# Softmax sums of an attention layer: ones products in four column groups of 32 in place of tile additions

## The chip, the cores and the metric

The kernel runs on one core of one Trainium2 chip. The metric is the device time of one execution in microseconds (us); lower is better. One execution was also taken with the hardware profiler, and all rows below come from it.

## The reference

Three layers follow each other on 896 tokens (2 batches of 448), 768 wide:

```python
scores = cap * np.tanh(scale * (q @ k.T) / cap)          # 24 heads, 448 x 448, head 64 wide
attn = np.exp(scores - max)
attn = attn / (attn.sum(axis=-1, keepdims=True) + 1e-9)
x = attn @ v                                             # then 896 x 768
x = moe(x)       # RMS norm, two products 768 -> 1536, SiLU gate, product 1536 -> 768
return moe2(x)   # product 768 -> 2048, PReLU, product 2048 -> 768
```

The change touches `attn.sum` alone: how the sum over keys is made and brought to the division.

## The kernel before, in words

**Tiling.** Two heads make a pair, and there are 12 pairs. Scores stand with keys on the 128 partitions and the 448 queries along the free dimension. A head has 448 keys: three tiles of 128 and a tail of 64. The tails of both heads share one tile, so a pair has seven tiles of exponentials in two bursts: b = 0 with four tiles, b = 1 with two full tiles and the shared tail. So there are 24 bursts, n = 0 to 23, burst n being (pair n // 2, half n % 2).

**One burst.** `qk` (L188) makes the scores of two groups of tiles on TensorE, each operand split in a high and a low part (`hi`, `lo`, made by `prep`, L174 and L175, on VectorE). `soft` does tanh (L198) and exp (L200) on ScalarE. `pv` (L211) multiplies with V; head 0 goes to columns 0 to 63 of the array and head 1 to 64 to 127. The PSUM pool of the scores has two buffers, one per group.

**The sums before.** `add_tiles` adds the full tiles of a pair to one tile per head on GpSimd (L223 after b = 0, L226 after b = 1), `add_tails` adds the halves of the tail tile on VectorE (L232), and `sums` multiplies the result with ones on TensorE (L238, one float32 product per head, 64 columns each; a float32 product is two passes, so four MATMULs a pair). `evac_u` copies the sum out of PSUM with the epsilon added (L270) and lays one row per head into `gt` by DMA (L273, on SyncE's queue). `recip` (L281 to L289) takes the reciprocal for a group of two pairs on 64 partitions, splits it in two parts and lays them into `r2` by two DMAs. `norm` spreads `r2` over partitions by a product (L314), multiplies (L315), and then squares and adds for the RMS norm, mostly on GpSimd (L296, L300, L304). The last pair has its own way: `sums_now` (L247) and `norm_now` (L322 to L324).

**Order.** The schedule is written by hand. Iteration n of the loop issues `qk` and `soft` of burst n, then `pv` of burst n - 1, then what `at(n, ...)` has put down for slot n, in the order in which it was put down. Every engine takes its instructions in this order, so a waiting instruction holds up all that its engine has behind it. Before, pair i has `add_tiles` in slots 2i + 1 and 2i + 2, `evac_o` (L262, frees the product with V) in slot 2i + 2, `add_tails` and then `sums` in slot 2i + 3, `evac_u` in slot 2i + 4, `recip` in slot 2i + 5 (every second pair), `norm` from slot 2i + 6. `prep` of pair i + 1 and the loads of pairs i + 1 (V) and i + 2 (Q and K) stand in slot 2i. Eight weight units are converted in between (L102 and L119 on ScalarE, L106 and L123 on VectorE, L114 on GpSimd). Slot 19 holds `rms(0)` (L333 to L337), slots 20 to 23 the six `xnorm` of batch 0 (L350 to L356, VectorE). After the last burst the products of the first layer begin (L368).

Of the kernel before, what the change touches and what calls it, by code (L numbers as in the profile page):

```python
# [7 lines left out]
F32 = mybir.dt.float32  # L8
# [6 lines left out]
ALU = mybir.AluOpType  # L15
PSUM = bass.MemoryType.PSUM

P = 128
B, H, S, D = 2, 12, 448, 64
# [13 lines left out]
RMS_EPS = 1e-6  # L33
SM_EPS = 1e-9
RP = 16
K3 = KD // 2
G1 = K1 // 2
G2 = K2N // 4
# [15 lines left out]
def attn_moe_kernel(ctx: ExitStack, tc: tile.TileContext, units, qk_in, v, sel, w, gvec, alpha, cap, out):  # L54
    nc = tc.nc
# [7 lines left out]
    sb = att.enter_context(tc.tile_pool(name="sb", bufs=2))  # L63
# [8 lines left out]
    eps_t = aconst.tile([P, 1], F32, name="eps_t")  # L72
    rms_b = aconst.tile([P, 1], F32, name="rms_b")
    ones = aconst.tile([P, P], F32, name="ones")
    half = aconst.tile([P, 2, D], F32, name="half")
# [80 lines left out]
    NPAIR = B * NP  # L156
# [22 lines left out]
    st, pt = {}, {}  # L179
# [19 lines left out]
            n += w  # L199
        nc.scalar.activation(out=t[:, :n], in_=t[:, :n], func=AF.Exp, scale=cap_t)  # L200

    oo, us, ut, ee, gt = {}, {}, {}, {}, {}

    def pv(i, b):
        t, vv = pt[i, b], vt[i]
# [9 lines left out]
        if b == 1:  # L215
            del hi[i], lo[i], vt[i]

    def add_tiles(i, b):

        t = pt[i, b]  # L220
        if b == 0:
            ut[i] = sb.tile([P, 2, S], F32, tag="ut", name="ut", bufs=2)
            nc.gpsimd.tensor_tensor(out=ut[i], in0=t[:, 0:2], in1=t[:, 2:4], op=ALU.add)  # L223
            del pt[i, 0]
        else:
            nc.gpsimd.tensor_tensor(out=ut[i], in0=ut[i], in1=t[:, 0:2], op=ALU.add)  # L226

    def add_tails(i):
        t = pt.pop((i, 1))
        for h in range(2):  # L230
            rows = slice(h * D, h * D + D)
            nc.vector.tensor_tensor(out=ut[i][rows, h], in0=ut[i][rows, h], in1=t[rows, 2], op=ALU.add)  # L232

    def sums(i):
        us[i] = ps_r.tile([P, 512], F32, tag="u", name="us")
        u = ut.pop(i)
        for h in range(2):
            nc.tensor.matmul(us[i][h * D:h * D + D, :S], ones[:, :D], u[:, h], start=True, stop=True)  # L238

    def sums_now(i):  # L240

        us[i] = ps_r.tile([P, 512], F32, tag="r", name="us")
        a, c = pt[i, 0], pt[i, 1]
        tiles = [a[:, 0], a[:, 1], a[:, 2], a[:, 3], c[:, 0], c[:, 1], c[:, 2], c[:, 2]]
        for n, t in enumerate(tiles):
            h = n % 2
            nc.tensor.matmul(  # L247
                us[i][h * D:h * D + D, :S], half[:, h] if n > 5 else ones[:, :D], t, start=n < 2, stop=n > 5,
                skip_group_check=True,
            )  # L250
# [4 lines left out]
    members = [[i, i + 1] for i in range(0, NPAIR - 2, 2)] + [[NPAIR - 2]]  # L255
# [8 lines left out]
    def evac_u(i):  # L264

        n, j = group[i]
        if j == 0:
            gt[n] = sb.tile([4 * RP, S // RP], F32, tag="gt", name="gt")
        u = sb.tile([P, S], F32, tag="us", name="us")
        nc.vector.tensor_scalar_add(u, us.pop(i)[:, :S], eps_t)  # L270
        for h in range(2):
            r0 = RP * (2 * j + h)
            nc.sync.dma_start(  # L273
                out=gt[n][r0:r0 + RP, :], in_=u[h * D:h * D + 1, :].rearrange("o (p s) -> o p s", p=RP)
            )

    def recip(n):
        t = gt.pop(n)
        w = 2 * len(members[n])
        m = slice(0, w * RP)  # L280
        nc.vector.reciprocal(out=t[m], in_=t[m])  # L281
        th = sb.tile([4 * RP, S // RP], F32R, tag="th", name="th")
        tl = sb.tile([4 * RP, S // RP], F32R, tag="tl", name="tl")
        nc.vector.tensor_copy(th[m], t[m])
        nc.vector.tensor_tensor(out=tl[m], in0=t[m], in1=th[m], op=ALU.subtract)
        rr = r2[n % 2]
        for r0, x in ((0, th), (32, tl)):
            row = rr[r0:r0 + w].rearrange("r (p s) -> r p s", p=RP)
            nc.sync.dma_start(out=row.bitcast(F32), in_=x[m].bitcast(F32))  # L289

    def square(i):
        b, p = divmod(i, NP)
        x = xf[b][:, p, :]
        if p == 0:
            s2[b] = [sb.tile([P, S], F32, tag="s2", name="s2", bufs=1)]
            nc.gpsimd.tensor_tensor(out=s2[b][0], in0=x, in1=x, op=ALU.mult)  # L296
        else:
            sq = sb.tile([P, S], F32, tag="sq", name="sq", bufs=2)
            if i < NPAIR - 4:
                nc.gpsimd.tensor_tensor(out=sq, in0=x, in1=x, op=ALU.mult)  # L300
            else:
                nc.scalar.activation(out=sq, in_=x, func=AF.Square)
            if p < NP - 1 and i < NPAIR - 2:
                nc.gpsimd.tensor_tensor(out=s2[b][0], in0=s2[b][0], in1=sq, op=ALU.add)  # L304
            else:
                s2[b].append(sq)
# [3 lines left out]
    def norm(i):  # L310
        b, p = divmod(i, NP)
        n, j = group[i]
        rps = ps_r.tile([P, 512], F32, tag="r", name="rps")
        nc.tensor.matmul(rps[:, :S], sel_t[:, j, :], r2[n % 2], start=True, stop=True)  # L314
        nc.vector.tensor_tensor(out=xf[b][:, p, :], in0=ee.pop(i), in1=rps[:, :S], op=ALU.mult)  # L315
        square(i)

    def norm_now(i):

        b, p = divmod(i, NP)  # L320
        u = sb.tile([P, S], F32, tag="us", name="us")
        nc.vector.tensor_scalar_add(u, us.pop(i)[:, :S], eps_t)  # L322
        nc.vector.reciprocal(out=u, in_=u)
        nc.vector.tensor_tensor(out=xf[b][:, p, :], in0=oo.pop(i)[:, :S], in1=u, op=ALU.mult)  # L324
        square(i)
# [3 lines left out]
    def rms(b):  # L329
        ms = ps_o.tile([P, 512], F32, tag="o", name="ms")  # L330
        parts = s2.pop(b)
        for n, t in enumerate(parts):
            nc.tensor.matmul(ms[:, :S], ones, t, start=n == 0, stop=n == len(parts) - 1)  # L333
        spare[b] = xpool.tile([P, K3, S], F32, tag="B22h", name="spare")
        rstd[b] = spare[b][:, 2]
# [6 lines left out]
    def first_operand(name):  # L342
        if name not in oper:
            oper[name] = [xpool.tile([P, K3, S], F32R, tag=f"{name}{p}", name=f"x{p}") for p in "hl"]
        return oper[name]

    def xnorm(i):
# [5 lines left out]
        if b == 0:  # L353
            h, l = first_operand("B21" if p >= K3 else "B11")
            nc.vector.tensor_copy(h[:, p % K3, :], x)
            nc.vector.tensor_tensor(out=l[:, p % K3, :], in0=x, in1=h[:, p % K3, :], op=ALU.subtract)  # L356

# [3 lines left out]
    def product(ps, u, name, first, rows=(0, 1)):  # L361

        wh, wl = h_t[u], l_t[u]
        xh, xl = oper[name]
        for r in rows:
            mm = [(a[:, r * K3 + k, :], x[:, k, :]) for a, x in ((wh, xh), (wl, xh), (wh, xl)) for k in range(K3)]
            for n, (lhs, rhs) in enumerate(mm):
                nc.tensor.matmul(  # L368
                    ps[:, r, :S], lhs, rhs, start=first and n == 0, stop=n == len(mm) - 1,
                    skip_group_check=True,  # L370
                )
# [14 lines left out]
    with tc.manual_schedule():  # L386
# [39 lines left out]
        def at(n, fn, *a):  # L426
            later.setdefault(n, []).append((fn, a))

        NA = len(bursts)
        last = NPAIR - 1  # L430
        for i in range(NPAIR):
            if i < last:
                at(2 * i + 4, evac_u, i)
        for i in range(NPAIR):
            if i < last:
                at(2 * i + 3, add_tails, i)
                at(2 * i + 3, sums, i)
        for i in range(NPAIR):
            at(2 * i, prep, i + 1)
            at(2 * i, load_raw, i + 2)  # L440
            at(2 * i, load_v, i + 1)
            if i < last:
                at(2 * i + 2, evac_o, i)
                for b in range(2):
                    at(2 * i + 1 + b, add_tiles, i, b)
                n, j = group[i]
                if j == len(members[n]) - 1 and n < len(members) - 1:
                    at(2 * i + 5, recip, n)
                    if n < len(members) - 2:
                        for m, i2 in enumerate(members[n]):  # L450
                            at(2 * i + 6 + m, norm, i2)
            if i == NP - 1:
                at(2 * i + 9, rms, 0)
                for m in range(NP):
                    at(2 * i + 10 + m * 2 // 3, xnorm, m)
# [14 lines left out]
        for n in range(NA):  # L470
            i, b = bursts[n]
# [5 lines left out]
            for fn, a in later.pop(n, []):  # L477
                fn(*a)
        sums_now(last)
        pv(*bursts[-1])  # L480
        for n in sorted(later):
# [4 lines left out]
        def pair_tile(pool, tag):  # L486
            return pool.tile([P, 2, 512], F32, tag=tag, name=tag)
# [14 lines left out]
                fn(*a)  # L502
        for g in range(2):
            pa[g] = pair_tile(ps_s, "s")
        norm_now(last)
        norm(last - 3)
        product(pa[0], ("g", 0, "A11"), "B11", True)
        recip(len(members) - 1)
        norm(last - 2)
        w_hi(("g", 0, "S1"))  # L510
        w_lo(("g", 0, "S1"))
# [489 lines left out]
```

## Time and profile before

| | |
|---|---|
| median of 3 runs | 653.34 us (652.91 to 654.76) |
| the profiled execution | 656.73 us |
| its span | 655.0 us |
| mean granted TensorE clock | 0.957 of 2.4 GHz |
| busy: PE, DVE, ACT, POOL | 593.3, 426.4, 341.0, 159.2 us |

The span and the profiled execution's own time differ by the launch, 1.7 us. PE is TensorE, DVE is VectorE, ACT is ScalarE, POOL is GpSimd and SPq is SyncE's queue; PEclk is the clock granted to TensorE as a share of 2.4 GHz, so that 0.5 is 1.2 GHz and a value between the two is a mean over a stretch. Matmuls are pipelined: one starts before the one ahead of it has ended, so the spacing of their starts says more than their durations. Engines work beside each other, so busy times do not add up to the span; the chain of waits is followed back from the last instruction, and only what stands on it sets the end.

### The profile page before, as it was taken

What the parts mean: (1) busy time and instruction counts of PE and PEld (TensorE: products, weight loads), DVE (VectorE), ACT (ScalarE), POOL (GpSimd) and SP (SyncE); (2) the same over time, 40 slices, a digit from 0 to 9 for tenths busy, and PEclk for the clock granted to TensorE, in tenths of its full rate; (3) what the DMA queues carried; (4) which work ended last, traced back from release to release, by engine and by line L of the source; (5) the groups of instructions that cost most, each with busy time, mean ns of one, the idle gap of its engine ahead of it and who ended that gap; (6) DMA issues with size and microseconds to landing.
All of it is one profiled execution on the core that took longest, in us unless ns stands there. A gap on an engine that the chain in (4) does not pass through costs nothing.

```text
span 655.0 us, 7086 instructions
## 1 busy us (share of the span) xinstructions
PE 593.3 (91%) x2793; PEld 481.4 (74%) x2793; DVE 426.4 (65%) x444; ACT 341.0 (52%) x389; POOL 159.2 (24%) x82
## 2 busy tenths in 40 slices
PE   6787766667899999999999999999989989999997
PEld 3233222223577899999999999999979979999996
DVE  4766656669778998777696344597986788613200
ACT  6596554536156465454566254358767687524101
POOL 3425376606050053423100003530233100000000
PEclk9997787778799999999999999999999999999999
DMA  8244321100030244441235437200441342632002
GB/s 267 101 143 131 107 94 49 46 17 2 1 145 1 96 136 154 145 143 50 94 99 193 145 116 266 101 0 1 144 146 49 101 152 87 198 118 104 1 0 85
DMA packets 16461, 65.99 MB, mean 101 GB/s; under 512 B 3500, under 2 KB 4012, under 8 KB 16428
## 3 DMA queue, kind: packets, MB, share of 16 engines
q1 hardware_dynamic: 16140, 65.41, 29.9%
q8 instruction: 22, 0.36, 0.2%
q0 software_dynamic: 144, 0.13, 0.1%
q14 instruction: 11, 0.09, 0.0%
q10 hardware_dynamic: 144, 0.00, 0.0%
HBM read 62.66 MB, written 2.75 MB: 100 GB/s over the span
## 4 chain that ended last, share of the span: by engine, by line
PE 75%; DVE 15%; issue 3%; POOL 3%; ACT 2%; DMA 1%; ACTq 0%; SPq 0%; DVEq 0%; POOLq 0%
PE s L368 17%; PE m L368 14%; PE s L637 5%; PE s L641 5%; PE s L639 5%; PE m L637 5%; PE m L641 5%; PE m L639 5%; PE us L238 3%; PE oo L211 3%; PE s L188 3%; DVE ut L232 2%; DVE b L550 2%; DVE wt L106 2%; DVE lo L175 2%
## 5 line engine op out<-in xcount | busy, mean ns | idle before, releaser
L123 DVE TENSOR_TENSOR wl<-wt,wh 128x768 fp32r<-128x768 f32 x98 | 108.5, 1113 | 96.5 <-ACT wh L119 95.4
L114 POOL TENSOR_TENSOR wt<-wt 128x768 f32<-128x768 f32 x40 | 88.6, 2222 | 253.1 <-DVE wt L106 147.1
L119 ACT CAST wh<-wt 128x768 fp32r<-128x768 f32 x98 | 81.3, 832 | 100.0 <-PE s L639 21.9
L102 ACT CAST top<-raw 128x768 f16<-128x768 bf16 x68 | 72.7, 1076 | 50.2 <-DVE wt L106 37.1
L106 DVE SCALAR_TENSOR_TENSOR wt<-raw,top 128x768 uint32<-128x768 uint32 x68 | 69.7, 1028 | 0.1
L198 ACT ACTIVATE pt<-s,cinv 128x896 f32<-128x896 f32 (+1 forms) x48 | 41.6, 907 | 41.8 <-PE s L188 40.5
L238 PE MATMUL us<-ut,ones 128*64 128x448 f32 x44 | 24.1, 795 | 38.6 <-DVE ut L232 38.6
L368 PE MATMUL s<-xh,wh 128*128 128x448 f32 x222 | 57.6, 368 | 0.9 <-DVE b L550 0.9
L368 PE MATMUL s<-xl,wh 128*128 128x448 f32 x222 | 57.2, 366 | 0.8 <-DVE xl L550 0.8
L368 PE MATMUL s<-xh,wl 128*128 128x448 f32 x222 | 57.1, 366 | 0.0
L637 PE MATMUL s<-ks,wh 128*128 128x448 f32 x176 | 50.8, 368 | 1.1 <-DVE b L878 1.1
L641 PE MATMUL s<-ks,wl 128*128 128x448 f32 x176 | 50.7, 367 | 0.0
L368 PE MATMUL m<-xh,wh 128*128 128x448 f32 x174 | 45.6, 371 | 2.4 <-ACT b L497 1.9
L637 PE MATMUL m<-ks,wh 128*128 128x448 f32 x160 | 45.8, 367 | 0.5 <-DVE b L550 0.5
L641 PE MATMUL m<-ks,wl 128*128 128x448 f32 x160 | 45.6, 366 | 0.0
L368 PE MATMUL m<-xl,wh 128*128 128x448 f32 x174 | 45.3, 369 | 0.0
L368 PE MATMUL m<-xh,wl 128*128 128x448 f32 x174 | 45.2, 369 | 0.0
L368 PEld LDWEIGHTS s<-xh,wh 128*128 128x128 f32 x222 | 41.5, 188 | 5.1 <-ACT wh L119 1.2
L368 PEld LDWEIGHTS s<-xl,wh 128*128 128x128 f32 x222 | 41.6, 188 | 4.5 <-DVE xl L550 1.1
L211 PE MATMUL oo<-pt,vt 128*64 128x448 f32 x192 | 43.6, 573 | 1.4 <-ACT pt L200 1.1
L238 PEld LDWEIGHTS us<-ut,ones 128*64 128x64 f32 x44 | 5.4, 172 | 53.3 <-DVE ut L232 53.3
L368 PEld LDWEIGHTS s<-xh,wl 128*128 128x128 f32 x222 | 41.7, 188 | 3.4
(136 smaller groups left out, 1056.0 us busy)
## 6 DMA issues: line engine op xcount, KB each, us to landing
raw<-w_in SPq DMA_DIRECT2D x68, 768.0 KB, 4.5
rw<-qk_in SPq DMA_DIRECT2D x11, 480.0 KB, 4.3
vt<-v_in SPq DMA_DIRECT2D x12, 256.0 KB, 4.2
out<-o SPq DMA_DIRECT2D x5, 448.0 KB, 2.5
out<-o SPq DMA_DIRECT2D x2, 224.0 KB
gt<-us SPq DMA_DIRECT2D x22, 1.8 KB, 1.7
rw<-qk_in SPq DMA_DIRECT2D x1, 256.0 KB
rw<-qk_in SPq DMA_DIRECT2D x1, 224.0 KB
```

The lines of the kernel that those rows point to most:

```text
L102: nc.scalar.copy(top_of[u].bitcast(F16)[:, 1::2], raw_t[u].bitcast(BF16)[:, 4:4 * UW + 4:4])
L106: nc.vector.scalar_tensor_tensor(out=f_t[u].bitcast(U32), in0=raw_t.pop(u).bitcast(U32)[:, 1:2 * UW + 1:2], scalar=13, in1=top_of.pop(u), ...
L114: nc.gpsimd.tensor_tensor(out=t, in0=f_t[a], in1=f_t[b], op=op)
L119: nc.scalar.copy(h_t[u], f_t[u].rearrange("p (k m) -> p k m", m=P))
L123: nc.vector.tensor_tensor(out=l_t[u], in0=f_t[u].rearrange("p (k m) -> p k m", m=P), in1=h_t[u], op=ALU.subtract)
L198: nc.scalar.activation(out=t[:, n:n + w], in_=st.pop((i, g))[:, :w, :S], func=AF.Tanh, scale=cinv)
L211: nc.tensor.matmul(oo[i][h * D:h * D + D, :S], vv[:, 2 * c + h, :], t[:, n, :], start=c == 0, stop=c == 3, skip_group_check=True,)
L238: nc.tensor.matmul(us[i][h * D:h * D + D, :S], ones[:, :D], u[:, h], start=True, stop=True)
L368: nc.tensor.matmul(ps[:, r, :S], lhs, rhs, start=first and n == 0, stop=n == len(mm) - 1, skip_group_check=True,)
L637: nc.tensor.matmul(dst[l], wh[:, o, :], xh[l], start=first, stop=False)
L639: nc.tensor.matmul(dst[l], wh[:, o, :], xl[l], start=False, stop=False)
L641: nc.tensor.matmul(dst[l], wl[:, o, :], xh[l], start=False, stop=fin)
```

## The change

The ones product is taken from the exponentials themselves. Eight products per pair (the tail tile twice, with weights that are one for the half of its head and zero for the other) go to four groups of 32 columns: head 0 to columns 0 and 32, head 1 to columns 64 and 96, so that each head has two partial sums. `add_tiles` and `add_tails` are gone. `sums` moves from slot 2i + 3 to 2i + 2, `evac_u` from 2i + 4 to 2i + 3, `recip` from 2i + 5 to 2i + 4. `evac_u` copies without the epsilon and issues four DMAs a pair for two; `recip` adds the two parts and the epsilon in one more VectorE instruction on 64 partitions. The last `recip` moves ahead of `norm_now`.

```diff
-    def add_tiles(i, b):
...
-            nc.gpsimd.tensor_tensor(out=ut[i], in0=t[:, 0:2], in1=t[:, 2:4], op=ALU.add)
-            del pt[i, 0]
-        else:
-            nc.gpsimd.tensor_tensor(out=ut[i], in0=ut[i], in1=t[:, 0:2], op=ALU.add)
-
-    def add_tails(i):
-        t = pt.pop((i, 1))
-        for h in range(2):
-            rows = slice(h * D, h * D + D)
-            nc.vector.tensor_tensor(out=ut[i][rows, h], in0=ut[i][rows, h], in1=t[rows, 2], op=ALU.add)
+    def tiles_of(i):
+        a, c = pt[i, 0], pt[i, 1]
+        return [a[:, 0], a[:, 1], a[:, 2], a[:, 3], c[:, 0], c[:, 1], c[:, 2], c[:, 2]]
 
     def sums(i):
+
         us[i] = ps_r.tile([P, 512], F32, tag="u", name="us")
-        u = ut.pop(i)
-        for h in range(2):
-            nc.tensor.matmul(us[i][h * D:h * D + D, :S], ones[:, :D], u[:, h], start=True, stop=True)
+        for n, t in enumerate(tiles_of(i)):
+            q = n % 2 * D + n // 2 % 2 * Q
+            nc.tensor.matmul(
+                us[i][q:q + Q, :S], half[:, n % 2, :Q] if n > 5 else ones[:, :Q], t, start=n < 4, stop=n > 3,
+                skip_group_check=True,
+            )
+        del pt[i, 0], pt[i, 1]
...
         if j == 0:
-            gt[n] = sb.tile([4 * RP, S // RP], F32, tag="gt", name="gt")
+            gt[n] = sb.tile([4 * RP, 2, S // RP], F32, tag="gt", name="gt")
         u = sb.tile([P, S], F32, tag="us", name="us")
-        nc.vector.tensor_scalar_add(u, us.pop(i)[:, :S], eps_t)
+        nc.vector.tensor_copy(u, us.pop(i)[:, :S])
         for h in range(2):
             r0 = RP * (2 * j + h)
-            nc.sync.dma_start(
-                out=gt[n][r0:r0 + RP, :], in_=u[h * D:h * D + 1, :].rearrange("o (p s) -> o p s", p=RP)
-            )
+            for k in range(2):
+                q = h * D + k * Q
+                nc.sync.dma_start(
+                    out=gt[n][r0:r0 + RP, k, :], in_=u[q:q + 1, :].rearrange("o (p s) -> o p s", p=RP)
+                )
...
-        nc.vector.reciprocal(out=t[m], in_=t[m])
+        f = sb.tile([4 * RP, S // RP], F32, tag="gf", name="gf")
+        nc.vector.scalar_tensor_tensor(
+            out=f[m], in0=t[m, 0], scalar=eps_t[m], in1=t[m, 1], op0=ALU.add, op1=ALU.add
+        )
+        nc.vector.reciprocal(out=f[m], in_=f[m])
...
-        for i in range(NPAIR):
-            if i < last:
-                at(2 * i + 4, evac_u, i)
-        for i in range(NPAIR):
-            if i < last:
-                at(2 * i + 3, add_tails, i)
-                at(2 * i + 3, sums, i)
+        for i in range(last):
+            at(2 * i + 2, sums, i)
+            at(2 * i + 3, evac_u, i)
...
-                for b in range(2):
-                    at(2 * i + 1 + b, add_tiles, i, b)
...
-                    at(2 * i + 5, recip, n)
+                    at(2 * i + 4, recip, n)
...
+        recip(len(members) - 1)
         norm_now(last)
         norm(last - 3)
         product(pa[0], ("g", 0, "A11"), "B11", True)
-        recip(len(members) - 1)
         norm(last - 2)
```

## Rows read from the trace of the kernel before

**Rows 1.** Windows: us, busy PE, PEld, DVE, ACT, POOL (instructions), PEclk, DMA share, GB/s.

```profile
52.00:134.36 82.36, 56.17 (x219) 23.62 (x215) 50.22 (x50) 41.12 (x38) 46.56 (x25) 0.79 0.24 76
193.70:655.00 461.30, 451.27 (x2196) 412.92 (x2196) 296.17 (x292) 235.51 (x283) 72.29 (x32) 0.99 0.31 104
```

**Rows 2.** Waits, 0 to 190 us: total, times, longest.

```profile
PE us L238 <- DVE ut L232: 38.6, 13, 5.6
```

**Rows 3.** Chain that ended last: start us, us, what.

```profile
26.00 1.68 PE oo L211 x8
...
48.84 0.42 PE rps L314
...
49.90 0.53 DVE ee L262
...
51.47 2.93 DVE lo L175
...
55.85 2.41 PE us L238 x4
...
58.93 2.54 PE s L188 x12
...
123.01 2.05 PE oo L211 x8
...
134.36 3.23 PE ms L333 x4
...
174.86 3.64 PE s L368 x18
```

**Rows 4.** Windows around one wait for the sums, columns as in the first group.

```profile
51.20:58.00 6.80, 3.46 (x12) 0.86 (x8) 5.19 (x5) 2.98 (x4) 2.18 (x1) 0.81 0.35 110
58.00:65.00 7.00, 7.00 (x31) 3.71 (x30) 2.62 (x4) 4.36 (x4) 5.17 (x4) 0.69 0.36 117
```

**Rows 5.** Timeline of TensorE in bursts 2 and 3: start us, us, what.

```profile
11.46 1.72 PE L211 MATMUL oo<-pt,vt 128*64 128x448 f32 x8
13.11 0.48 PE L188 MATMUL s<-hi 64*128 64x448 f32 x2
...
14.54 1.72 PE L211 MATMUL oo<-pt,vt 128*64 128x448 f32 x8
16.20 0.47 PE L188 MATMUL s<-hi 64*128 64x448 f32 x2
...
17.95 1.72 PE L211 MATMUL oo<-pt,vt 128*64 128x448 f32 x8
21.18 0.96 PE L238 MATMUL us<-ut,ones 128*64 128x448 f32 x2 [1.50 <-DVE ut L232]
```

**Rows 6.** Timeline of ScalarE in bursts 2 and 3.

```profile
14.19 1.89 ACT L198 ACTIVATE pt<-s,cinv 128x896 f32<-128x896 f32 x2
...
17.81 1.51 ACT L198 ACTIVATE pt<-s,cinv 128x896 f32<-128x896 f32 x2
...
20.67 1.04 ACT L102 CAST top<-raw 128x768 f16<-128x768 bf16 x1
```

**Rows 7.** Groups by line and shape, 0 to 190 us: busy, mean ns, idle before.

```profile
L232 DVE TENSOR_TENSOR ut<-ut,pt 64x448 f32<-64x448 f32 x22 | 24.1, 1094 | 6.2 <-POOL ut L226 5.9
...
L281 DVE RECIPROCAL gt<-gt 64x28 f32<-64x28 f32 x5 | 1.5, 306 | 0.1
```

**Rows 8.** Timeline of VectorE in slot 2.

```profile
16.86 0.65 DVE L174 CAST hi<-rw 128x960 fp32r<-128x960 f32 x1
17.54 1.16 DVE L175 TENSOR_TENSOR lo<-rw,hi 128x960 fp32r<-128x960 f32 x1
```

**Rows 9.** Line L273, the DMAs of the sums: ns min/median/max, first and last start.

```profile
L273 SPq DMA_DIRECT2D gt<-us x22: 508/578/1003, 25.3 to 170.8; - x22
...
DMA to landing us min/median/max: 1.6/1.7/4.1
```

**Rows 10.** Timeline of ScalarE around slot 19.

```profile
144.88 1.91 ACT L198 ACTIVATE pt<-s,cinv 128x896 f32<-128x896 f32 x2
```

More of the change, by code (lines that the diff above doesn't have):

```diff
@@ L35 @@
 RP = 16
+Q = 32
 K3 = KD // 2
@@ L200, in soft @@
         nc.scalar.activation(out=t[:, :n], in_=t[:, :n], func=AF.Exp, scale=cap_t)
-    oo, us, ut, ee, gt = {}, {}, {}, {}, {}
+    oo, us, ee, gt = {}, {}, {}, {}
     def pv(i, b):
@@ L216, in pv @@
             del hi[i], lo[i], vt[i]
-    def add_tiles(i, b):
-        t = pt[i, b]
-        if b == 0:
-            ut[i] = sb.tile([P, 2, S], F32, tag="ut", name="ut", bufs=2)
-            nc.gpsimd.tensor_tensor(out=ut[i], in0=t[:, 0:2], in1=t[:, 2:4], op=ALU.add)
-            del pt[i, 0]
-        else:
-            nc.gpsimd.tensor_tensor(out=ut[i], in0=ut[i], in1=t[:, 0:2], op=ALU.add)
-    def add_tails(i):
-        t = pt.pop((i, 1))
-        for h in range(2):
-            rows = slice(h * D, h * D + D)
-            nc.vector.tensor_tensor(out=ut[i][rows, h], in0=ut[i][rows, h], in1=t[rows, 2], op=ALU.add)
+    def tiles_of(i):
+        a, c = pt[i, 0], pt[i, 1]
+        return [a[:, 0], a[:, 1], a[:, 2], a[:, 3], c[:, 0], c[:, 1], c[:, 2], c[:, 2]]
     def sums(i):
         us[i] = ps_r.tile([P, 512], F32, tag="u", name="us")
-        u = ut.pop(i)
-        for h in range(2):
-            nc.tensor.matmul(us[i][h * D:h * D + D, :S], ones[:, :D], u[:, h], start=True, stop=True)
+        for n, t in enumerate(tiles_of(i)):
[5 more added lines that the diff above has]
+        del pt[i, 0], pt[i, 1]
     def sums_now(i):
         us[i] = ps_r.tile([P, 512], F32, tag="r", name="us")
-        a, c = pt[i, 0], pt[i, 1]
-        tiles = [a[:, 0], a[:, 1], a[:, 2], a[:, 3], c[:, 0], c[:, 1], c[:, 2], c[:, 2]]
-        for n, t in enumerate(tiles):
+        for n, t in enumerate(tiles_of(i)):
             h = n % 2
@@ L280, in recip @@
         m = slice(0, w * RP)
-        nc.vector.reciprocal(out=t[m], in_=t[m])
+        f = sb.tile([4 * RP, S // RP], F32, tag="gf", name="gf")
[3 more added lines that the diff above has]
+        nc.vector.reciprocal(out=f[m], in_=f[m])
         th = sb.tile([4 * RP, S // RP], F32R, tag="th", name="th")
         tl = sb.tile([4 * RP, S // RP], F32R, tag="tl", name="tl")
-        nc.vector.tensor_copy(th[m], t[m])
-        nc.vector.tensor_tensor(out=tl[m], in0=t[m], in1=th[m], op=ALU.subtract)
+        nc.vector.tensor_copy(th[m], f[m])
+        nc.vector.tensor_tensor(out=tl[m], in0=f[m], in1=th[m], op=ALU.subtract)
         rr = r2[n % 2]
```

## The prediction

> **What bounds the kernel now.** I read first the busy time and granted clock by stretch, then the waits, then the chain, then single timelines of the attention stage. From 193.7 us to the end TensorE is busy 451.27 of 461.30 us at a clock of 0.99 [rows 1]; nothing of the change touches that stretch, so I take it as fixed and moved as a block. In the attention stage from 52 to 134 us TensorE is busy 56.17 of 82.36 us at 0.79 of its clock [rows 1]: neither full nor fast. The longest wait on the chain is the sums product, which waits 38.6 us in all, 13 times, for the additions of the tails on VectorE [rows 2]. The chain shows one round: after the product that spreads the reciprocals, VectorE evacuates, splits Q and K (the low part takes 2.93 us), converts weights, adds the tails, and at 55.85 the sums start, with the rest of TensorE's queue behind them [rows 3]. So every pair goes once from TensorE through VectorE's whole queue (and through GpSimd's additions) and back before the next scores can be made. The wait has a second price: TensorE was busy 3.46 of 6.80 us in the stretch that holds one of them, and in the next 7.0 us, fully busy, it had a mean clock of 0.69, so most of that ran at the lower level of 1.2 GHz [rows 4].
>
> I mark three points on the chain: the product with V in iteration 4 starts at 26.00, the one in iteration 18 at 123.01, the first layer's products at 174.86 [rows 3]. Between the first two lie seven pairs, 97.0 us, 13.9 us each; the last stage is 51.9 us.
>
> **Part by part.**
>
> *The wait.* The new sums read the exponentials, which the product with V just ahead of them on TensorE has read too. They wait for nothing new but their PSUM bank, which `evac_u` of the pair before frees some three quarters of a pair earlier. So the 38.6 us go, and TensorE is held by what is late next: its own work, ScalarE, or the split of Q and K.
>
> *The sums' own price.* Sixteen passes a pair for four. Nothing in the trace has 32 columns. The nearest row is the product with V: eight passes in two column groups, 11.46 to the next start at 13.11, 1.65 us, while the two passes of one lone head take 0.96 [rows 5]: four such couples one after the other would be 3.8 us, not 1.65, so the two groups run fully beside each other, four rounds of 0.41. If four groups do so too, the sums take the same four rounds, 1.65 us; if only two do, eight rounds, 3.2; if none does, sixteen, 6.6. I take 1.65, because in the nearest row no time at all was lost between groups; the other two are for the range and a rival. At the full clock the old sums took two rounds, some 0.9 us, so the price is 0.75 us a pair, all of it on TensorE.
>
> The Trainium skill (TensorE: Matmul & The Clock Gate, Measured speedup vs the span model) gives 2.38 for three column tiles of 32 columns, not 3. At that efficiency four groups would give 3.2, an estimate of 2.1 us for the sums and 4 to 5 us more over eleven pairs; no run here shows it. The Trainium skill (TensorEngine Tiling (Array Packing), Key Properties) also says that a change of tiling mode drains the array, which speaks against one more mode per pair. In this trace the products with V and the scores alternate between two modes all along, and the hand-over is inside the 1.65 us.
>
> *TensorE's round.* At the full clock the scores of an even burst take 1.43 us (13.11 to 14.54), of an odd one at most 1.75 (16.20 to 17.95, of which a little is waiting); I take 1.65. The products with V are 1.65 each [rows 5], the sums 1.65, the spreading product 0.42 [rows 3]. Together 1.43 + 1.65 + 3.30 + 1.65 + 0.42 = 8.4 us a pair.
>
> *ScalarE's round.* An even burst takes 3.62 us (14.19 to 17.81) and an odd one 2.86 (to 20.67): 6.5 us a pair, plus one weight conversion of 1.04 in two pairs of three and some smaller ones [rows 6], about 7.5. It is below TensorE's 8.4 and mostly hidden by it.
>
> *VectorE.* The tail additions, 24.1 us [rows 7], and GpSimd's additions go; VectorE's own work may shorten too: the low part takes 1.16 us at 17.54 and 2.93 at 51.47 [rows 8, 3], which I put down to GpSimd's additions beside it, and I let both prices stand as bounds. VectorE keeps about 5.5 us a pair, but in a fixed order. Two places are tight. (a) Every fourth slot it must first finish `norm`, which waits for sums and spreading product, then evacuate (0.55 [rows 3]) and split (1.8 to 3.0): ready 6.8 to 8.1 us after the product with V began, where TensorE wants the split at 7.4. (b) Two slots later `recip` now stands ahead of evacuation and split, one slot of VectorE work behind its `evac_u`. Its four DMAs are issued one after the other, 4 x 0.58, and the last lands 1.7 later [rows 9]: 4.0 us, of which one or two are filled by other work. Then the reciprocal, 0.31 [rows 7], and three instructions of its size, one of them new, 0.85 in all; evacuation and split: ready at 16.0 to 17.3 where TensorE wants it at 15.9. I take 0.5 and 0.7 us of waiting in two pairs, so 16.8 + 1.2 = 18.0, **9.0 us a pair** for 13.9. The copy without epsilon saves nothing that matters, and the added DMAs on SyncE's queue, 1.2 us a pair, are hidden: what stands behind them, the loads of Q, K and V, is needed two slots later. The exponentials' buffers are held a slot longer on paper, but the next scores stand behind the sums on TensorE anyway: nothing.
>
> *The clock.* With waits of a microsecond instead of 3.5 to 6, I take the full clock throughout.
>
> *The sum.* Up to iteration 4: the sums of pair 0 cost 1.65, and no wait; its product with V starts at 22.3 instead of 26.0: 3.7 us. Seven pairs: 97.0 - 63.0 = 34. The last stage: from iteration 18 to the end of the RMS product (two products with V, sums, one burst's scores, each 1.65, and the RMS product at half of its 3.23 us, since it ran at the lower clock [rows 3]) 8.2 us; then ScalarE is held by the table change, the root and the weight part that waits for VectorE's long reciprocal, as now (the product ends at 137.6, the next tanh is at 144.9, 7.3 us [rows 3, 10]; 6.7 without the `recip` that moves away); then four bursts, 18 us, with VectorE's `xnorm` beside them and no longer ahead of the sums. The last `recip` now stands ahead of `norm_now` and waits for the four DMAs of the tenth pair; this holds the second `norm` and the product behind it by about 2 us. 8.2 + 6.7 + 18 + 2 = 34.9 for 51.9: 17. Together 3.7 + 34 + 17 = 54.7 us off the profiled execution's 656.73, which gives 602. The median of the runs is 3.4 below that execution; against it 653.3 - 54.7 gives **599**.
>
> **The rivals.**
>
> *Only two column groups overlap, or VectorE's waits are longer than I take them.* The sums are then 3.2 us and TensorE's round 10.0; or split and `recip` cost 2 us more in two pairs. For it: no row has four groups, and `recip` meets a DMA that once took 4.1 us [rows 9]. Against it: two groups lose nothing. 1 to 1.5 us a pair over ten pairs, with a few more in the last stage: 610 to 620.
>
> *No overlap of the 32-column groups, so that the change does not do what it says.* Sums of 6.6, a round of 13.3 with no wait for additions: 0.6 us a pair gained, some 8 in all, about 645.
>
> *The clock stays at 1.2 GHz, and it is slower than before.* At that level the scores of an even burst took 2.54 [rows 3], 1.8 times as long, so the round of 8.4 becomes 15.3, against 13.9 now. Place: the seven pairs and the last stage. Price: 1.4 us a pair and a last stage no shorter, about +12, 665. It decides once the low level holds for over three quarters of the stage (9.0 and 15.3 mixed to 13.9); before, a mean of 0.79 means some two fifths. For it: the low level is there now, and four narrow groups leave the array as busy by time as before but no more. Against it: it followed the waits, which go [rows 4].
>
> **How the numbers follow.** Forecast 0.70 (588 to 610), the first rival 0.18, no overlap 0.06, the low clock 0.06 (a part of it no slower than before). The lower end, 588, is TensorE's 8.4 us a pair with no VectorE wait (another 6 us) and 5 off the last stage. The upper, 620, takes in two overlapping groups. That leaves out about 0.15. A measurement of this kernel can tell about 0.3% from no change. Faster by more: 0.93, within it 0.02, slower 0.05.
>
> **What would show it.** Right: no wait of the sums for VectorE; eight products of 32 columns in some 1.7 us; seven pairs between the same two marks in 60 to 66 us; clock near 1.0 until 80 us; low parts near 1.2 us; after the first layer's products start, the same 480 us as before. Wrong: starts of the sums' passes 0.4 us apart one by one (no overlap); scores that wait long for the split, or a reciprocal that waits over 4 us for its DMAs; a clock of 0.5 in half of the stage; a longer stretch behind the attention.

## The result, and the profile after

The changed kernel took 606.5 us in the median of four runs (603.2 to 611.1) beside 654.1 of the kernel before on the same chip: a ratio of 0.926, 95% interval 0.919 to 0.934. Measured once more, on the chip of the last four experiments, it was 606.7 and 0.923 [0.918, 0.928]. The forecast was 599 in a range of 588 to 620, so size and sign held. The profiled execution took 603.23 us; the forecast against the profiled execution of before had been 602.

The same three marks on TensorE as before. First the chain of the changed kernel, with the product with V in iteration 4 (before at 26.00 [rows 3]) and two of the sums:

```profile
16.17 1.64 PE us L228 x16
...
22.48 1.68 PE oo L212 x8
...
42.31 1.64 PE us L228 x16
```

Then TensorE's timeline, with the product with V in iteration 18 (before at 123.01), the first product of the first layer (before at 174.86, both in [rows 3]):

```profile
87.08 1.73 PE L212 MATMUL oo<-pt,vt 128*64 128x448 f32 x8
...
125.16 0.77 PE L366 MATMUL s<-xh,wh 128*128 128x448 f32 x3
```

Seven pairs take 64.6 us for 97.0, the last stage 38.1 for 51.9, and iteration 4 begins 3.5 us earlier: 49.7 us by the first product. The rest of the span, 480.1 us before, is 476.3: another 3.8, in a part that the change does not touch (below). The windows (us, busy PE, PEld, DVE, ACT, POOL, PEclk, DMA share, GB/s) answer to [rows 1]:

```profile
52.00:80.00 28.00, 25.25 (x161) 10.51 (x157) 17.85 (x25) 21.52 (x21) 10.55 (x7) 1.00 0.43 141
80.00:100.00 20.00, 19.01 (x120) 7.89 (x115) 12.64 (x17) 15.06 (x15) 6.68 (x4) 1.00 0.24 78
100.00:140.00 40.00, 34.71 (x175) 20.59 (x168) 32.56 (x46) 23.24 (x26) 12.93 (x9) 0.91 0.18 67
```

TensorE, busy 68% of its time at a mean clock of 0.79 before, is busy 90 to 95% of it at 2.4 GHz from 52 to 100 us; from 100 to 140 us the mean clock is 0.91. The waits (total, times, longest; 0 to 140 us) have nothing left of the 38.6 us of [rows 2]; the longest new one is VectorE's, for the DMAs of the sums ahead of `recip`:

```profile
DVE gf L276 <- DMA gt<-us: 13.7, 5, 4.2
...
PE s L189 <- ACT pt L199: 5.1, 3, 4.2
...
PE s L189 <- DVE lo L176: 1.6, 4, 0.6
```

And by group (busy, mean ns, idle before) VectorE's split, which the change does not touch, has become shorter. First the kernel before (0 to 175 us), then the changed one (0 to 145 us):

```profile
L175 DVE TENSOR_TENSOR lo<-rw,hi 128x960 fp32r<-128x960 f32 x11 | 22.9, 2085 | 0.4
L174 DVE CAST hi<-rw 128x960 fp32r<-128x960 f32 x11 | 12.7, 1153 | 0.6 <-DMA rw<-qk_in 0.6
```

```profile
L176 DVE TENSOR_TENSOR lo<-rw,hi 128x960 fp32r<-128x960 f32 x11 | 14.4, 1309 | 0.4
L175 DVE CAST hi<-rw 128x960 fp32r<-128x960 f32 x11 | 8.8, 803 | 0.3 <-DMA rw<-qk_in 0.3
```

### The profile page after: what moved, and what is told of

It is laid out like the page before. It is cut to its first block, busy times and chain, and to the rows that moved or that the text cites. A ratio compares the mean times of both kernels' runs of the same rounds, so it can differ in the third digit from the quotient of the medians.

```text
span 601.5 us, 7318 instructions
## 1 busy us (share of the span) xinstructions
PE 574.0 (95%) x2925; PEld 473.2 (79%) x2925; DVE 387.1 (64%) x428; ACT 340.5 (57%) x389; POOL 110.1 (18%) x60
## 4 chain that ended last, share of the span: by engine, by line
PE 74%; DVE 16%; ACT 4%; DMA 3%; issue 2%; SPq 1%; ACTq 0%; DVEq 0%
PE s L366 18%; PE m L366 15%; PE s L633 6%; PE s L629 6%; PE s L631 6%; PE m L629 5%; PE m L633 5%; PE m L631 5%; PE oo L212 2%; DVE b L542 2%; PE s L189 2%; DVE lo L176 2%; DMA gt<-us 2%; DVE wt L107 1%; PE m L378 1%
## 5 line engine op out<-in xcount | busy, mean ns | idle before, releaser
L115 POOL TENSOR_TENSOR wt<-wt 128x768 f32<-128x768 f32 x40 | 91.6, 2296 | 250.4 <-DVE wt L107 144.9
L107 DVE SCALAR_TENSOR_TENSOR wt<-raw,top 128x768 uint32<-128x768 uint32 x68 | 68.2, 1006 | 0.0
L366 PE MATMUL s<-xh,wh 128*128 128x448 f32 x222 | 57.5, 368 | 0.9 <-DVE b L542 0.9
L212 PE MATMUL oo<-pt,vt 128*64 128x448 f32 x192 | 42.2, 561 | 1.9 <-ACT pt L201 1.8
L631 PE MATMUL s<-b,wh 128*128 128x448 f32 x144 | 41.2, 365 | 0.0
L631 PE MATMUL m<-b,wh 128*128 128x448 f32 x144 | 40.9, 365 | 0.0
```

The source lines that it names most:

```text
L107: nc.vector.scalar_tensor_tensor(out=f_t[u].bitcast(U32), in0=raw_t.pop(u).bitcast(U32)[:, 1:2 * UW + 1:2], scalar=13, in1=top_of.pop(u), ...
L115: nc.gpsimd.tensor_tensor(out=t, in0=f_t[a], in1=f_t[b], op=op)
L212: nc.tensor.matmul(oo[i][h * D:h * D + D, :S], vv[:, 2 * c + h, :], t[:, n, :], start=c == 0, stop=c == 3, skip_group_check=True,)
L366: nc.tensor.matmul(ps[:, r, :S], lhs, rhs, start=first and n == 0, stop=n == len(mm) - 1, skip_group_check=True,)
L631: nc.tensor.matmul(dst[l], wh[:, o, :], xl[l], start=False, stop=False)
```

## The experiments

The marks of all kernels, from TensorE's timeline of the profiled execution. "Block" is the start of the first product of the part that no kernel here changes (L380 before, 193.70 us); the ratio is to the kernel before on the same chip. The profile of one execution is the finer ruler for a stage; the ratio is the one with an interval.

| kernel | median us | ratio [95%] | seven pairs | block starts |
|---|---|---|---|---|
| before | 654 to 658 | 1 | 97.0 | 193.7 |
| changed | 606.5, 606.7 | 0.926 [0.919, 0.934], 0.923 [0.918, 0.928] | 64.7, 64.4 | 144.6, 144.2 |
| e1 two groups | 611.9 | 0.934 [0.927, 0.941] | 69.6 | 150.9 |
| e2 additions kept | 648.9 | 0.989 [0.983, 0.995] | 90.4 | 186.6 |
| e3 before, filled | 646.3 | 0.986 [0.979, 0.993] | 92.2 | 185.6 |
| e4 old slots | 618.5 | 0.941 [0.934, 0.948] | 69.1 | 154.8 |
| e5 GpSimd's load | 626.2 | 0.954 [0.948, 0.959] | 74.8 | 163.8 |
| e6 holds | 613.8 | 0.934 [0.927, 0.940] | 67.2 | 149.4 |
| e7 recip later | 600.8 | 0.917 [0.912, 0.922] | 61.4 | 140.9 |
| e8 last recip back | 605.4 | 0.923 [0.917, 0.929] | 66.4 | 144.5 |
| e9 tails' load | 610.7 | 0.930 [0.924, 0.936] | 67.0 | 150.0 |
| e10 both recips | 603.2 | 0.917 [0.912, 0.923] | 61.3 | 140.5 |
| e11 unit earlier | 601.0 | 0.917 [0.911, 0.922] | 61.3 | 140.9 |

### e1: two groups of 64 columns

```diff
-            q = n % 2 * D + n // 2 % 2 * Q
+            q = n % 2 * D
...
-                us[i][q:q + Q, :S], half[:, n % 2, :Q] if n > 5 else ones[:, :Q], t, start=n < 4, stop=n > 3,
+                us[i][q:q + D, :S], half2[:, n % 2] if n > 5 else ones2, t, start=n < 2, stop=n > 5,
```

> The changed kernel with the eight ones products in two column groups of 64 (weights 0.5, so that both partial rows of a head add up to its sum) in place of four groups of 32; DMAs, slots and recip as changed. Theory (TensorE's own round of 8.4 us a pair now sets the pace, and four groups overlap fully): the sums take 3.2 instead of 1.65 us, 1.55 us a pair longer on the path, less what VectorE's waits absorb: 12 to 17 us slower than the changed kernel, about 619. Rival (VectorE's order sets the pace, TensorE has slack): less than 6 us slower.

The product with V and the sums of one pair in TensorE's timeline, and what follows them:

```profile
42.53 1.72 PE L214 MATMUL oo<-pt,vt 128*64 128x448 f32 x8
44.09 2.42 PE L230 MATMUL us<-pt,ones 128*64 128x448 f32 x12
46.34 0.92 PE L230 MATMUL us<-pt,half 128*64 128x448 f32 x4
47.19 0.47 PE L314 MATMUL rps<-r,sel_t 128*128 128x448 f32 x1
```

From 44.09 to the next start at 47.19 is 3.1 us, where the four groups take 1.64: nearly twice as long with half the groups. The product with V ahead of the sums hands over after 1.56 us (42.53 to 44.09) instead of 1.65, because here both have the shape 128*64. So a pair has 1.37 us more for TensorE, and eleven pairs 15; the block starts 6.3 us later, the median is 5.4 higher, and the ratio is 0.7% higher, with intervals that overlap. So some 40% of what TensorE does more is on the path. The theory's 12 to 17 us did not come; the rival's "less than 6" is met by the median and just missed by the block. That fits a pace that TensorE and VectorE set by turns.

### e2: the additions kept beside the new sums

```diff
+            at(2 * i + 3, add_tails, i)
...
+                for b in range(2):
+                    at(2 * i + 1 + b, add_tiles, i, b)
```

`add_tiles` and `add_tails` are those of before; their result is not used.

> The changed kernel with the old tile additions on GpSimd and VectorE kept in their old slots beside the new sums; their result is read by nothing. It tells the wait from the load. Theory (what was won is that TensorE no longer waits for the additions): at least two thirds of the gain stays, so below 622; VectorE's longer queue and slower splits cost 5 to 15 us. Rival (what was won is the load taken off VectorE and GpSimd, which stretched VectorE's splits): more than half of the gain goes, above 630.

My theory fell, and hard; the rival's "above 630" holds. TensorE waits for no addition any more, and yet only 7.1 of 49.1 us (193.7 to 186.6) are won. The waits (0 to 166 us) show where the old wait went:

```profile
PE s L189 <- DVE hi L175: 12.4, 2, 7.2
ACT pt L199 <- DVE ut L234: 11.8, 3, 5.7
...
ACT pt L199 <- POOL ut L226: 6.6, 3, 3.4
```

The scores wait for late splits, and ScalarE's tanh waits 18.4 us for buffers of exponentials that the additions still hold. (The reverse, the load gone and the wait kept, was not run, so 7 and 42 us are prices in this order.) The timelines of VectorE and GpSimd in the same kernel show why VectorE is late:

```profile
61.44 1.41 DVE L292 SCALAR_TENSOR_TENSOR gf<-gt,eps_t 64x28 f32<-64x28 f32 x1 [2.92 <-DMA gt<-us]
62.89 0.32 DVE L295 RECIPROCAL gf<-gf 64x28 f32<-64x28 f32 x1
63.24 1.75 DVE L298 CAST th<-gf 64x28 fp32r<-64x28 f32 x1
65.03 2.00 DVE L299 TENSOR_TENSOR tl<-gf,th 64x28 fp32r<-64x28 f32 x1
```

```profile
60.73 2.09 POOL L226 TENSOR_TENSOR ut<-pt 128x896 f32<-128x896 f32 x1
62.89 2.07 POOL L228 TENSOR_TENSOR ut<-ut,pt 128x896 f32<-128x896 f32 x1
64.92 2.07 POOL L226 TENSOR_TENSOR ut<-pt 128x896 f32<-128x896 f32 x1
```

A subtraction of 28 elements, 0.18 us elsewhere, takes 2.00 us: it ends at 67.03, GpSimd's addition at 66.99. The cast ends at 64.99, the addition ahead at 64.96. The first ends at 62.85, with 62.82. Only the reciprocal goes through in its 0.32 us. So three small VectorE instructions each lasted until the GpSimd addition beside them ended. The Trainium skill (SBUF — State Buffer, Who interferes with whom) says that these two engines share a pair of memory ports under an exclusive lock, held for a whole instruction, for VectorE's casts in its fast modes and its operations with two operands from SBUF; the rows agree.

### e3: the kernel before, with its wait filled

```diff
+        if i > 1:
+            for n in range(8):
+                h = n % 2
+                nc.tensor.matmul(us[i][h * D:h * D + D, :S], ones[:, :D], hi[i + 1][:, h * S:h * S + S].bitcast(F32), start=True, stop=True, skip_group_check=True)
```

> The kernel before with eight ones products on the Q and K operands, overwritten at once, put on TensorE ahead of each pair's sums from pair 2 on, in the time in which it waits for the tails. It prices the clock alone, for the wait stays. Theory (the wait had a second price, the 1.2 GHz level behind it): granted clock above 0.95 from 50 to 170 us instead of 0.79, and 8 to 18 us faster than before, 636 to 646. Rival (a faster TensorE only waits longer): within 4 us of before.

Windows of the filled kernel, then of the kernel before, each from 52 us to the product with V in iteration 18:

```profile
52.00:118.36 66.36, 56.58 (x274) 23.04 (x273) 45.52 (x44) 32.57 (x31) 41.03 (x23) 0.95 0.28 87
```

```profile
52.00:122.94 70.94, 48.41 (x189) 20.94 (x185) 42.82 (x44) 32.54 (x31) 40.10 (x23) 0.79 0.25 77
```

The useless products raise the mean clock from 0.79 to 0.95, and the kernel is 1.4% faster, the block 8.1 us earlier. So the low level behind the wait had its price, about a sixth of the whole gain: at the lower edge of what I expected. The clock was not full everywhere (0.93 from there to the first layer's products), so the whole price may be a little higher.

### e4: the products in the slots of before

```diff
-            at(2 * i + 2, sums, i)
-            at(2 * i + 3, evac_u, i)
+            at(2 * i + 3, sums, i)
+            at(2 * i + 4, evac_u, i)
...
-                    at(2 * i + 4, recip, n)
+                    at(2 * i + 5, recip, n)
```

> The changed kernel with sums, evac_u and recip back in the slots of before (one later each), still as eight products of the exponentials. Theory (the exponentials' three buffers are now held until the sums): the tanh of each odd burst has to wait for a buffer until product with V and sums of that iteration are done, some 2 to 3.5 us of ScalarE's and then TensorE's time a pair, 15 to 35 us slower than the changed kernel, 620 to 640. Rival (the slot alone matters little, as the next scores stand behind the sums anyway): within 6 us of the changed kernel.

The mechanism is as expected; ScalarE's waits (0 to 170 us) have it eleven times, once a pair:

```profile
ACT pt L199 <- PE us L228: 24.2, 11, 3.4
```

The size is not: 24.2 us of waiting moved the block by 10.3 and the median by 12, below the 15 to 35 that I gave; part of it was probably ScalarE's slack, which no run shows by itself. The slot move is therefore a part of the change of its own, worth about a fifth of it.

### e5, e6, e9: the additions taken apart

GpSimd's load alone (e5, on a tile of its own), the holds alone (e6, additions of one column that read the exponentials), VectorE's tails alone (e9, on a tile of its own):

```diff
+    def add_tiles(i, b):
+        nc.gpsimd.tensor_tensor(out=ut, in0=ut, in1=ut, op=ALU.add)
...
+            nc.gpsimd.tensor_tensor(out=ut[i][:, :, :1], in0=t[:, 0:2, :1], in1=t[:, 2:4, :1], op=ALU.add)
...
+            nc.vector.tensor_tensor(out=ut[rows, h], in0=ut[rows, h], in1=ut[rows, 1 - h], op=ALU.add)
```

> The changed kernel with GpSimd's two additions a pair kept in their old slots, but on a tile of their own that nothing else touches: GpSimd's load without a reader, without a held buffer and without the tails on VectorE. Theory (of the 42 us that the kept additions cost, most is VectorE's work beside a busy GpSimd, whose instructions the kept additions stretched: the splits from 1.3 to 1.8 us, the small ones of recip from 0.4 to 1.0): 15 to 25 us slower than the changed kernel, ratio to before 0.95 to 0.965. Rival (it was the exponentials' buffers, held until the additions): within 6 us of the changed kernel.

> The changed kernel with the old additions cut to one column each, still reading the exponentials in their old slots: almost no load, but each buffer of exponentials is held until GpSimd and VectorE come to it in their queues. Theory of the held buffers: ScalarE's tanh waits for them as it did with the kept additions (18 us in all there), 12 to 25 us slower than the changed kernel, ratio to before 0.945 to 0.965. Rival (load and stretch alone): within 6 us of the changed kernel.

> The changed kernel with VectorE's two tail additions a pair kept in their old slot, on a tile of their own that nothing else touches: VectorE's load alone, GpSimd idle as in the changed kernel. Theory (VectorE's order is co-bound with TensorE, and what was taken off it is worth its time only where its queue is late): 22 x 0.62 = 13.6 us of work, of which between a half and all shows: 7 to 14 us slower than the changed kernel, ratio to before 0.937 to 0.95. Rival (VectorE has room, and only GpSimd's stretching of its instructions hurts): within 4 us.

GpSimd's load alone, 43.7 us of additions, costs 19.2 us (the block at 163.8 for 144.6), 3% of the time and as expected, though nothing reads what it does. Its trace has the split back near the durations of before, 2085 and 1153 ns (groups of VectorE, 0 to 150 us), where the changed kernel has 1309 and 803:

```profile
L176 DVE TENSOR_TENSOR lo<-rw,hi 128x960 fp32r<-128x960 f32 x11 | 21.3, 1937 | 0.4
L175 DVE CAST hi<-rw 128x960 fp32r<-128x960 f32 x11 | 12.4, 1125 | 0.0
```

Without GpSimd, VectorE's own tails (14.6 us of work in e9) cost 5.4 us, and the split stays at 1309 ns:

```profile
L224 DVE TENSOR_TENSOR ut<-ut 64x448 f32<-64x448 f32 x22 | 14.6, 665 | 0.2
L176 DVE TENSOR_TENSOR lo<-rw,hi 128x960 fp32r<-128x960 f32 x11 | 14.4, 1309 | 0.4
```

The holds alone cost 4.8 us by the block; the tanh waits only 1.6 us for a tile so released, for a small addition is quickly done. The intervals of e6 and e9 overlap with those of the changed kernel (0.934 and 0.930 for 0.923 to 0.926), so their sizes are those of one profile each. The theory of held buffers and that of a VectorE with hardly any room both gave too much. Of their rivals, "within 6" fits e6 by the block (4.8) and not by the median (7.3), and "within 4" is missed by e9 a little (5.4 and 4.2). Only that GpSimd's load is the largest of the three is clear of noise. The three sum to 29.4 of the 42.0 us that the kept additions cost together. The remaining 12.6 come only when all are there. In e2 the slow additions hold buffers longer and the mean clock is back at 0.86 between 52 and 113 us; what each of these costs was not separated.

### e7, e8, e10, e11: what the change gives away

```diff
-                    at(2 * i + 4, recip, n)
+                    at(2 * i + 5, recip, n)
...
-        recip(len(members) - 1)
         norm_now(last)
...
+        recip(len(members) - 1)
...
-            s0 = 3 + 9 * j // 4
+            s0 = 3 + 9 * j // 4 - (j == 7)
```

e7 has the first part, e8 the second, e10 both, e11 the third on top of both.

> The changed kernel with recip of the first five groups back one slot (2i + 5), evac_u where it is. Theory (recip at the head of VectorE's slot waits for its four DMAs, 13.7 us in five waits, and holds up evacuation and splits behind it): VectorE's wait for these DMAs falls below 3 us and the seven pairs between the marks take 61 to 63 us instead of 64.7; 2 to 4 us faster than the changed kernel. Rival (TensorE's own work fills that time anyway, or the spreading product now waits for the later reciprocals): within 1.5 us, or slower.

> The changed kernel with the last recip back behind norm_now and the first product, as before. Theory (ahead of norm_now it waits 2.2 us for its DMAs with norm_now's 4.3 us behind it, which holds the second spreading product): the stretch from the first product of the layer to the end of its first part falls by 1.5 to 3 us. Rival (the products ahead hide it, and the later reciprocals hold the last norm): within 1 us.

> The changed kernel with both recip moves taken back: the first five one slot later, the last behind norm_now and the first product. If the two add up (5.7 us in the medians for the first, 1.6 us between the marks for the second): 6 to 8 us faster than the changed kernel, ratio to before 0.912 to 0.918. Rival (the second was noise): 0.917 as with the first alone.

> As with both recips taken back, and the eighth weight unit converted one slot earlier, so that ScalarE's copy of it in slot 19 no longer waits behind VectorE's long reciprocal of the RMS norm ahead of the next tanh. Theory (that wait, 3.8 us on ScalarE and 4.2 us on TensorE, and the 1.2 GHz stretch behind it set the pace of slots 19 to 21): 3 to 6 us faster than with the recips alone. Rival (VectorE's xnorm is late there anyway): within 1.5 us.

Their base, the changed kernel once more on the same chip as e9, e10 and e11:

> The changed kernel as it is, on the same chip as the three others of this call, as their base. Expected ratio to before 0.92 to 0.93.

e7 does what was expected. VectorE's wait for the DMAs falls from 13.7 to 1.1 us, the seven pairs from 64.7 to 61.4, and with them the block by 3.7; the median falls by 5.7, a ratio of 0.917 for 0.926 or 0.923. The intervals of the two still overlap slightly, but e10 and e11, which contain the edit, have 0.917 too and the same 61.3 us. TensorE is now all but full (windows of e7):

```profile
22.00:52.00 30.00, 28.58 (x189) 11.55 (x185) 16.85 (x26) 27.77 (x27) 3.01 (x3) 1.00 0.52 156
52.00:80.00 28.00, 27.39 (x177) 11.95 (x175) 18.43 (x26) 23.86 (x24) 12.79 (x9) 1.00 0.52 167
```

e8 is a null. The last stage and the stretch to the block together fall from 57.5 to 55.8 us, but only 0.4 of this lies behind the first product, where 1.5 to 3 had been expected, and 1.2 ahead of it. Its seven pairs took 1.7 more, with a stretch at 1.2 GHz in them, and the block starts where it did. The same edit on top of e7 (e10) shortens the two together by 0.4 us only, and e10 is no faster than e7. e11 is a null for a reason that its trace names. ScalarE's timeline has the tanh of slot 20 (before in [rows 10]), first in the changed kernel, then in e11:

```profile
104.51 1.91 ACT L199 ACTIVATE pt<-s,cinv 128x896 f32<-128x896 f32 x2
```

```profile
97.21 1.91 ACT L199 ACTIVATE pt<-s,cinv 128x896 f32<-128x896 f32 x2
```

It begins 7.3 us earlier, 3.4 of them from the shorter pairs, but TensorE then stands elsewhere (waits of TensorE in e11, 0 to 130 us):

```profile
PE rps L312 <- DMA r<-tl: 4.2, 2, 3.8
```

With `recip` a slot later, the group of pairs 6 and 7 stands in slot 19 behind the RMS norm's long reciprocal, and the spreading product waits for its DMA. e10 has the same wait:

```profile
PE rps L312 <- DMA r<-tl: 4.7, 3, 4.0
```

So in e10 and e11 the later `recip` takes the place of the wait that the earlier unit removes; `recip` of this one group in its earlier slot and the rest later would be the next thing, and was not tried. e7, e10 and e11 are faster than both kernels of the study, about 1% below the changed one, with intervals that still overlap with its own.

## Why the prediction was right, and where it was not

**The sums' price: right.** Sixteen passes in four groups take 1.64 us, as eight in two do; forecast 1.65. None of the rivals with less overlap holds. By the efficiency that the Trainium skill gives for three groups (TensorE: Matmul & The Clock Gate, Measured speedup vs the span model) an estimate was 2.1; the measurement decides, and here four groups lost nothing. The added change of tiling mode does have a price, a small one: the product with V hands over after 1.65 us to another shape and after 1.56 to sums of its own shape (e1), so about 0.1 us a change and 1 us over eleven pairs, inside the 1.64 and 1.65. (The prediction's 0.96 us for a lone head's two passes is a duration and not a spacing, so its 3.8 us for four such couples is too long; that two groups overlap stands, since e1 has sixteen passes in 3.1 us.)

**The pace: right, 9.2 us a pair for 9.0.** Iteration 4 starts its product with V at 22.48 (forecast 22.3). One of the signs that the prediction names for being wrong did come: `recip` waits for its DMAs 13.7 us in five waits, up to 4.2, where 4.0 less one or two of other work had been put. The price on the path was still small: forecast at 0.7 us in two pairs, 2.5 over the seven pairs, it is 3.2 by e7 (64.6 to 61.4). With it gone the pace is 8.8, close to the 8.4 of TensorE alone.

**The last stage: 38.1 us for 34.9.** The mis-sized term is the block on ScalarE in slots 19 and 20: the tanh of slot 20 starts 17.4 us after the mark, where 8.2 + 6.7 = 14.9 had been put. The first part took 9.2 us, up to the end of the RMS product, and the second 8.2. ScalarE's timeline shows why the second is longer. Before:

```profile
130.31 1.28 ACT L336 ACT_TABLE_LOAD   x1
137.62 0.64 ACT L336 ACTIVATE spare<-ms,rms_b 128x448 f32<-128x448 f32 x1 [6.02 <-PE ms L333]
```

After, with the end of the RMS product on TensorE:

```profile
95.37 0.92 PE L331 MATMUL ms<-sq,ones 128*128 128x448 f32 x2
```

```profile
96.61 1.28 ACT L334 ACT_TABLE_LOAD   x1
97.91 0.63 ACT L334 ACTIVATE spare<-ms,rms_b 128x448 f32<-128x448 f32 x1
```

Before, ScalarE loaded the table for the root while TensorE still waited for the sums, so the 7.3 us from which the prediction takes its 6.7 held no such load. After, ScalarE has no idle time there: its exponentials end at 96.60, the load starts 0.3 us behind the RMS product, and the root 1.6 us behind it. The wait that went had hidden this work. Waiting for this tanh, TensorE is without work for 4.2 us, and its clock falls to 1.2 GHz: 0.51 from 103.3 to 110.2 us, in which it is busy 4.63. From the tanh to the first product it took 20.7 us for 20. The 2 us for the last `recip` are not borne out: with it moved back the last stage is 1.2 us shorter in e8, and no shorter in e10 than in e7.

**The cause: mis-sized, though the sum came out.** The prediction says of the 38.6 us that they "go", because the new sums no longer read the additions, and lets the shorter splits stand as a mere bound. e2 shows that ending that reading alone wins 7 us: the wait passes to the splits and to ScalarE's buffers. The other 42 come from the additions' not being there. e5 puts 19 of these on GpSimd's additions beside VectorE (43.7 us there, 52.8 in the kernel before); how they hold VectorE up is shown by the two engines' ends in e2's timeline. So the term that was mis-sized is "VectorE's own work may shorten too": it is the largest item that the runs separate. The pace was still right because it was built bottom up, from the work that stays on TensorE and VectorE, and not from the wait that goes.

**The clock: right until 100 us** (1.00), and not in the last stage. By itself it was worth 8 us (e3).

**Queues and buffers.** SyncE's longer queue cost nothing outside `recip`: VectorE's split waits 0.3 us in all for the loads of Q and K. The buffers cost nothing because the sums moved; left where they were, the products would have lost 10 us to them (e4).

**The part behind: not fixed, and that was luck.** From the block on it took 461.3 us before and 456.9 after, with the same instructions. About 1.9 us of the 4.4 arise near 489 us of the kernel before: a wait of 1.92 us instead of 1.53 for ScalarE's L497 (L489 in the changed kernel), and the clock behind it. The same stretch before, then after:

```profile
489.20:493.20 4.00, 4.00 (x14) 3.60 (x13) 4.00 (x5) 0.64 (x2) 2.06 (x2) 0.60 0.49 148
```

```profile
440.00:444.00 4.00, 4.00 (x21) 3.63 (x20) 4.00 (x4) 2.17 (x4) 2.39 (x2) 1.00 0.55 184
```

Most of the rest is a pace of TensorE that differs between the profiled executions of these kernels (last section). So 4.4 us of the 53.5 between the two profiles are not shown to be the change's. Up to the first product the change won 49.7 us where 54.7 were forecast; that the profiled execution came within 1.2 us of the forecast 602 is owed to the part behind, which no term of the prediction had. The medians stand 3 us above the profiled execution; the same pace may be the reason, which is not shown, since the other executions have no profile.

## What to carry to other kernels

An engine's wait in the trace tells who was last, not what its removal is worth: build the new pace from the work that stays, and price the work that goes on every engine, above all GpSimd's beside VectorE. When a reduction can be taken by ones products from tiles that TensorE reads anyway, four groups of 32 columns make eight float32 products as cheap as four in two groups. Then look at what was moved nearer to its own DMAs: one slot of distance for `recip` was worth about another percent. And ask what other engines did during a wait that goes: here a table load had been hidden in it.

## What was not expected of the hardware

A change of the matmuls' shape on TensorE has a price of about 0.1 us: a product with V is followed after 1.65 us by another shape and after 1.56 by its own (e1).

Three small VectorE instructions of about 0.2 us took 1.4 to 2.0 us and ended 0.03 to 0.04 us after the GpSimd addition that ran beside them, one after the other (e2).

TensorE's pace in the unchanged block differs between executions at the same granted clock. The window from 200 to 260 us, in the middle of that block, fully busy and at 1.00, of the changed kernel and of e6:

```profile
200.00:260.00 60.00, 60.00 (x297) 55.63 (x297) 43.31 (x46) 30.15 (x38) 23.22 (x11) 1.00 0.36 119
```

```profile
200.00:260.00 60.00, 60.00 (x292) 54.51 (x291) 43.16 (x46) 27.66 (x36) 26.31 (x12) 1.00 0.43 143
```

297 and 292 matmuls, so 202 and 205 ns each. The starts in the block are mostly either 202 to 203 or 206 to 207 ns apart, and an execution keeps to one of the two for hundreds of matmuls: e4, e6 and e10 run to about the 1350th of 2196 at the wider spacing and then at the narrower, the kernel before, e2 and e11 have the wider one in the last 550, e9 nearly throughout, the changed kernel hardly at all. The block took 456.9 to 457.7 us in six of the profiles, 461.3 to 464.3 in five, 458.7 to 460.0 in three, with no relation to the edits that could be seen (both ends occur among the variants of the changed kernel). What sets the spacing stays open, and so does whether one and the same kernel can have both: the changed kernel's two profiles, 456.9 and 457.2 us, are both at the narrower. The spread of the block, 7.4 us, is about as large as the 1% by which runs of one kernel differ here; that it is their cause is not shown.
